# Score products of 28 and of 30 rows: one row count for all of them

## The chip, the cores and the metric

The kernel runs on one core of a Trainium2 chip. The metric is device time in microseconds (us). TensorE (PE in the profile) multiplies; it loads one operand as weights (PEld) and streams the other. VectorE (DVE), ScalarE (ACT) and GpSimd (POOL) do the elementwise work, and SyncE (SP) issues nearly all DMAs.

## The reference

Two attentions over the same x (2048 positions, 448 columns, 16 heads of 28), mixed by a gate. One looks at 8 positions at distance 2; the other, where nearly all of the time goes, is a full softmax attention:

```python
def _B_ref(x, wqkv, wo):
    qkv = (x @ wqkv).reshape(B, S, 3, H, Dh).transpose(2, 0, 3, 1, 4)
    q, k, v = qkv[0], qkv[1], qkv[2]
    scores = jnp.einsum("bhqd,bhkd->bhqk", q, k) * (Dh ** -0.5)
    p = _softmax(scores, axis=-1)
    o = jnp.einsum("bhqk,bhkd->bhqd", p, v)
    return o.transpose(0, 2, 1, 3).reshape(B, S, D) @ wo

g = _sigmoid((x * gate_w).sum(-1, keepdims=True))
return g * _A_ref(x, A_wqkv, A_wo) + (1 - g) * _B_ref(x, B_wqkv, B_wo)
```

`_A_ref` is the local attention. Everything is float32.

## The kernel before

[...]

**Three stages.** First x is multiplied with the weights (`project`, `project_halves`): the first ten tiles with all 128 rows of the array (line 320), the rest with two halves of 64 rows at a time (line 325). The high and low parts of queries and keys go to DRAM (`qk_hi`, `qk_lo`). The main stage, from about 248 us to 820 us, is the full attention with the local one beside it, and the last multiplies with `wo` (`op_tile`).

**Units, heads and strips.** A unit `u` is four heads (group `g`) by 512 queries, 16 units in all; a unit has 16 steps, one for each 128 keys, so 256 steps `st`. The four heads of a group lie in four strips of 32 partitions, head `h` in rows 32h to 32h + 27. Rows 28 and 29 of a strip are used in one kind of product: the keys' high tiles `KH` are filled with 1.0 (`init_kh`) before keys are loaded, and the queries' high tile `QH` gets two rows there (`load_nm`), the high and low part of the negative maximum of each query. So a high product of 30 rows yields scores with the maximum subtracted. The low tiles `QL` and `KL` have nothing in rows 28 and 29, and their products take 28 rows. `QH` and `QL` are made for each unit in a pool of two rotating buffers (`load_part`, called by `load_q` 4 steps before the unit, which then also loads the maxima's rows). There are three `KH` and two `KL` tiles, which are loaded again as groups come and go (`load_k`).

**Maxima's products.** The maxima are found beforehand from high by high products alone (`s1_mm`, line 149): those beside the projections take two strips at once (64 rows, the strip that is not wanted holding zeros in `QP`), those beside the main stage 28 rows. VectorE reduces each bank to its maximum (`s1_max`, line 155).

**A step.** `scores` writes products in a fixed order. A letter names the bank, a digit the term (0: `KH` by `QH`, 1: `KH` by `QL`, 2: `KL` by `QH`; `s0` to `s2` are the maxima's products):

```python
WITH = "10 20 s0 11 21 30 00 12 22 31 01 s1 s2 32 02".split()
```

Two ScalarE exponentials (line 1047) take two banks each. The three pairs of banks rotate: the pair that holds `s1` and `s2` in one step takes the products `30` and `00` in the next. Once no maxima are left, `ALONE` is the order, with the 12 products of the scores. After the products of a step, `do_av` (line 1008) multiplies the exponentials of the step before with the values, in 32 columns of the array for each head.

**The other engines.** Lists with costs and due steps spread the local attention's operations on GpSimd and VectorE over the steps; the same holds for the maxima's small steps (`max_parts`, `max_turn`, `max_store`). At the start, GpSimd sets constants and two `KH` tiles, VectorE clears three small tiles, and TensorE multiplies zeros (`warm`, line 220) until the first x and weights are there. `main_tiles`, called in the first step of the main stage, makes `KH2` and `KL1` in memory that the projections used.

Of the kernel before, what the change touches and what calls it, by code (L numbers as in the profile page):

```python
# [8 lines left out]
F32 = mybir.dt.float32  # L9
F32R = mybir.dt.float32r  # L10
# [5 lines left out]
S, D, H, DH = 2048, 448, 16, 28  # L16
NB, NJ, NG = 4, 16, 4
W, DIL = 8, 2
HALO = (W - 1) * DIL
SCALE = DH ** -0.5  # L20
NU = NG * NB
NMX = 192
# [3 lines left out]
def gated_mix_kernel(ctx: ExitStack, tc: tile.TileContext, xT, xn, gw, wA, wB, woAB, out):  # L26
    nc = tc.nc
# [3 lines left out]
    qk_hi = dram.tile([2 * D, S], F32R, name="qk_hi")  # L31
    qk_lo = dram.tile([2 * D, S], F32R, name="qk_lo")
# [11 lines left out]
    cp = ctx.enter_context(tc.tile_pool(name="cp", bufs=1))  # L44
    sp = ctx.enter_context(tc.tile_pool(name="sp", bufs=2))
# [27 lines left out]
    KL = [cp.tile([128, S], F32R, name="KL0")]  # L73
    MX = cp.tile([128, NMX], F32, name="MX")

    QP = [[cp.tile([128, 512], F32R, name=f"QP{i}{k}") for k in range(2)] for i in range(2)]

    def init_kh(t):
        nc.gpsimd.memset(t.bitcast(F32), 1.0)

    def pair(name):
        return pp.tile([128, 2, 512], F32, tag="P", name=name)

    half = {}
# [10 lines left out]
    def dma_r(dst, src):  # L99
        nc.sync.dma_start(dst.bitcast(F32), src.bitcast(F32))  # L100
# [4 lines left out]
            r = D + 112 * g + DH * h  # L105
            dma_r(t[32 * h:32 * h + DH, c], src[r:r + DH, c])

    def load_part(u, name, src):
        g, b = divmod(u, NB)
        t = sp.tile([128, 512], F32R, name=name)  # L110
        for h in range(4):
            r = 112 * g + DH * h
            dma_r(t[32 * h:32 * h + DH, :], src[r:r + DH, 512 * b:512 * b + 512])
        return t

    Qs = {}

    def load_q(u, low=True):
        Qs[u] = load_part(u, "QH", qk_hi), load_part(u, "QL", qk_lo)
        if low:  # L120
            load_nm(u)

    def load_nm(u):
        for i in range(2):
            dma_r(Qs[u][0][DH + i::32, :], nm[u][16 * i:16 * i + 16, :].rearrange("(h q) c -> h (q c)", h=4))
# [8 lines left out]
    def load_qhi(u):  # L134
        g, b = divmod(u, NB)
        qhis[u] = QP[u % 2]
        for h in range(4):
            r = 112 * g + DH * h
            dma_r(qhis[u][h % 2][32 * h:32 * h + DH, :], qk_hi[r:r + DH, 512 * b:512 * b + 512])

    def s1_mm(n, bank, half=False):
        u, i = divmod(n, 64)
        qs, kc, h = i // 16, i // 4 % 4, i % 4
        if u == 0:
            qs, kc = i // 8 % 4, 2 * (i // 32) + i // 4 % 2
        if i == 0 and u + 1 < NU:
            load_qhi(u + 1)
        r = slice(64 * (h // 2), 64 * (h // 2) + 64) if half else slice(32 * h, 32 * h + DH)
        nc.tensor.matmul(bank, qhis[u][h % 2][r, 128 * qs:128 * qs + 128],  # L149
                         KH[u // NB % 3][r, 512 * kc:512 * kc + 512], start=True, stop=True)  # L150

# [56 lines left out]

    for t in KH:
        init_kh(t)  # L210
    t0 = pair("t0")[:, 0, :]
    nc.vector.memset(t0, 0.0)
    nc.vector.memset(zt, 0.0)
    nc.vector.memset(omt, 0.0)

    zero = nc.const_aps.tensor(0.0, [128, 512], F32).bitcast(F32R)

# [8 lines left out]
    if True:  # L226
# [210 lines left out]
        nc.scalar.activation(zt, zt, AF.Exp)  # L437
        for t in QP[0]:
            nc.scalar.activation(t, t0, AF.Copy)
        r, t = xst[:, 0, 0:3, :], xst[:, 0, 3, :]  # L440
# [45 lines left out]
        for n, t in enumerate(tiles[:-1]):  # L486
# [4 lines left out]
            for w in splits:  # L491
                i, k = (n - splits[w][0]) * splits[w][1], splits[w][1]
# [19 lines left out]
            if n == 4:  # L512
                for t in QP[1]:
                    nc.scalar.activation(t, t0, AF.Copy)
# [20 lines left out]
            if parts and parts[0][0] <= n:  # L535
                _, u, t = parts.pop(0)
                max_store(u, max_turn(t))
            if finished and n < len(tiles) - 3:
                u = finished.pop(0)
# [10 lines left out]
            if n == 70:  # L550
                r = sp.tile([128, 32], F32, name="omr")
# [57 lines left out]
    def main_tiles():  # L609
        nonlocal mp, pm, maskt, actx, a1, a2, a3  # L610
        hctx.close()
        mp = ctx.enter_context(tc.tile_pool(name="mp", bufs=1))

        KH.append(mp.tile([128, S], F32R, name="KH2"))
        KL.append(mp.tile([128, S], F32R, name="KL1"))
        init_kh(KH[2])
        pm = ctx.enter_context(tc.tile_pool(name="pm", bufs=8))

        maskt = mp.tile([128, W, NJ, 2], F32, name="maskt")
        nc.gpsimd.memset(maskt, 0.0)  # L620
        for st, g, t, src in ((12, 2, KH[2], qk_hi), (30, 1, KL[1], qk_lo), (72, 2, KL[0], qk_lo),
                              (100, 3, KH[0], qk_hi), (136, 3, KL[1], qk_lo)):
            at("end", st, lambda g=g, t=t, src=src: load_k(g, t, src))
        for w in range(1, W):
            nc.gpsimd.memset(maskt[0:1, w, 0:DIL * w, :], -1e9 / SCALE)

        actx = ExitStack()
        a1 = actx.enter_context(tc.tile_pool(name="a1", bufs=1))
        a2 = actx.enter_context(tc.tile_pool(name="a2", bufs=2))
        a3 = actx.enter_context(tc.tile_pool(name="a3", bufs=5))  # L630
        for nme in ("k", "v"):
            for i in range(2):
                t = a1.tile([128, HALO + NJ, 56], F32, name=f"{nme}t{i}")
                kvt[nme, i] = t
# [4 lines left out]
    def a_load(c, nme):  # L639
# [3 lines left out]
        else:  # L643
            t = kvt[nme, c % 2]
            i = 1 if nme == "k" else 2
            nc.sync.dma_start(t[:, 0:HALO, :], a_prev[i][c, :, NJ - HALO:NJ, :])
            nc.sync.dma_start(t[:, HALO:, :], a_own[i][c])

    def a_score(c, w):
        if w == 0:  # L650
            Lt[c] = a2.tile([128, W, NJ, 2], F32, name="L", bufs=3)
        p = a3.tile([128, NJ, 56], F32, tag="prod", name="prod")
        nc.gpsimd.tensor_tensor(out=p, in0=qt[c], in1=kvt["k", c % 2][:, HALO - DIL * w:HALO - DIL * w + NJ, :],  # L653
                                op=ALU.mult)
# [10 lines left out]
    def a_softmax(c, i):  # L665
# [12 lines left out]
        elif i == 4:  # L678
            nc.scalar.activation(L, L, AF.Exp, scale=SCALE)  # L679
        elif i in (5, 6):  # L680
# [17 lines left out]
    def a_av(c, w, part):  # L698
# [3 lines left out]
        if part == 0:  # L702
# [3 lines left out]
            else:  # L706
# [3 lines left out]
                out=dst.rearrange("p j (h d) -> p j h d", d=DH),  # L710
                in0=kvt["v", c % 2][:, HALO - DIL * w:HALO - DIL * w + NJ, :].rearrange("p j (h d) -> p j h d", d=DH),
                in1=Lt[c][:, w, :, :, None].to_broadcast([128, NJ, 2, DH]), op=ALU.mult)
# [111 lines left out]
    def split_wo(k):  # L824
        if not wo:
            spare = [t[:, D * i:D * i + D] for t in (KH[1], KH[2], KL[0]) for i in range(4)] + [t[:, :D] for t in QP[0]]
            wo.extend((spare[:7], spare[7:]))
# [138 lines left out]
    for u in range(NU - 1):  # L966
        f = NJ * (u + 1)
        h = (16, 18)
# [50 lines left out]
    def scores(u, kt, cur):  # L1019
        g = u // NB  # L1020
        n = s1c[0]
        k = min(3, s1e - n)
        qh, ql = Qs[u]
        ks = slice(128 * kt, 128 * kt + 128)
        one, mine, other = ring
        ring[:] = (one, other, mine) if k else (other, one, mine)
        bank = {"1": one[:, 0, :], "2": one[:, 1, :], "3": mine[:, 0, :], "0": mine[:, 1, :],
                "s0": T1, "s1": other[:, 0, :], "s2": other[:, 1, :]}
        for tok in WITH if k else ALONE:
            if tok[0] == "s":  # L1030
                i = int(tok[1])
                if i < k:
                    s1_mm(n + i, bank[tok])
                if i == 0:
                    s1_max(n, 1, T1)
                elif i == 2 and k > 1:
                    s1_max(n + 1, k - 1, other[:, 0:k - 1, :])
                continue
            a, t = tok[0], int(tok[1])
            h = (int(a) + n) % 4  # L1040
            r = slice(32 * h, 32 * h + (DH + 2 if t == 0 else DH))
            nc.tensor.matmul(bank[a], (KH[g % 3], KH[g % 3], KL[g % 2])[t][r, ks], (qh, ql, qh)[t][r, :], start=(t == 0), stop=(t == 2))  # L1042
            if t == 2 and a in "20":
                if len(exps) < 5:
                    probs.append(pair("P"))
                p = probs[len(exps) % 5]
                e = nc.scalar.activation(p, one if a == "2" else mine, AF.Exp, scale=SCALE).ins  # L1047
                for o in exps[-5:-4]:
                    tc.declare_no_dep(e, o, query=mybir.DependencyQuery.ANY_SYNC,
                                      reason="PE has read what it wrote, and this one waits for PE")  # L1050
                for o in maxs[-4:]:
                    tc.declare_no_dep(e, o, reason="PE waited for it and the exponential waits for PE")
                exps.append(e)
                cur[(h + 3) % 4], cur[h] = p[:, 0, :], p[:, 1, :]
                yield len(cur)

    for u in range(NU):
        g, b = divmod(u, NB)
        for kt in range(NJ):
# [23 lines left out]
            if finished:  # L1083
                v = finished.pop(0)
                t = counted(lambda: max_parts(v, (lambda f: at("end", st + 1, f)) if v < NU - 1 else None))
# [25 lines left out]
    u = NU - 1  # L1111
# [30 lines left out]
```

## Time and profile before

| | |
|---|---|
| median of 3 runs | 896.43 us (896.38 to 896.9) |
| the profiled execution | 896.69 us, span of its records 894.9 us |
| TensorE busy | 890.2 us (99%) |
| VectorE, ScalarE, GpSimd busy | 740.5, 642.4, 638.7 us |
| exponentials (line 1047) | 512, 1023 ns each |
| maxima (line 155) | 470, 954 ns on average |
| weighted sums (line 1008) | 2048 records, 605 ns on average |

The span runs from the first record of the program to the last one; the execution's time has 1.8 us more around it. Matmuls are pipelined, and a record's duration holds its flight through the array and, for the first of a burst, its wait for weights: so durations add up to more than the time that passes, and the distance of two starts says more than a duration. A line of a timeline gives start and duration in us, engine, line, operation, the tiles written and read, shapes and a count; a group's line ends in busy us, mean ns, and idle time before it with what ended it.

### The profile page before, as it was taken

How to read it: one execution, taken by the hardware profiler on the slowest of the kernel's cores; microseconds unless marked ns; L12 is line 12 of the kernel's file. 1: busy time of each engine (PE TensorE's matmuls, PEld its weight loads, DVE VectorE, ACT ScalarE, POOL GpSimd, SP SyncE). 2: the span in 40 equal slices, each digit the busy share in tenths (PEclk: the TensorE clock that was granted, in tenths of full speed). 3: DMA queues.
4: the chain of work that ended last, by engine and by line, in shares of the span. 5: the costliest groups of instructions: out<-in, count | busy, mean ns of one | idle time of the engine just before them, and what ended most of it. 6: DMA issues, size and time to landing. Idle time of an engine off the chain costs nothing.

```text
span 894.9 us, 20516 instructions
## 1 busy us (share of the span) xinstructions
PE 890.2 (99%) x8312; PEld 533.4 (60%) x8312; DVE 740.5 (83%) x962; ACT 642.4 (72%) x766; POOL 638.7 (71%) x505
## 2 busy tenths in 40 slices
PE   9999999999999999999999999999999999999998
PEld 7889999999954444444444444444444444434997
DVE  6688999999979999999999999999999999832220
ACT  7456434343378898898988989989888898897220
POOL 1499846464459789998999989999999799701000
PEclk9999999999999999999999999999999999999999
DMA  8886403454372241225225222533121322437781
GB/s 267 277 267 186 151 12 84 135 142 121 103 248 66 89 139 46 67 61 156 71 56 143 86 62 86 128 96 98 45 64 32 89 43 49 104 78 214 192 265 52
DMA packets 114038, 104.51 MB, mean 117 GB/s; under 512 B 75240, under 2 KB 82280, under 8 KB 113160
## 3 DMA queue, kind: packets, MB, share of 16 engines
q1 hardware_dynamic: 113512, 102.42, 40.7%
q8 instruction: 65, 1.06, 0.5%
q10 hardware_dynamic: 432, 0.79, 0.3%
q14 instruction: 29, 0.24, 0.1%
HBM read 62.20 MB, written 40.96 MB: 115 GB/s over the span
## 4 chain that ended last, share of the span: by engine, by line
PE 99%; ACT 0%; issue 0%; ACTq 0%
PE T L1042 31%; PE av L1008 28%; PE r L325 15%; PE r L320 8%; PE T L886 8%; PE r L149 4%; PE T L149 4%; PE r L220 0%; PE av L472 0%; ACT P L1047 0%; ACT res L895 0%; ACT onhi L943 0%; ACT L L679 0%; ACTq L943 0%
## 5 line engine op out<-in xcount | busy, mean ns | idle before, releaser
L1047 ACT ACTIVATE P<-T 128x1024 f32<-128x1024 f32 x512 | 496.8, 1023 | 59.6 <-PE T L1042 57.9
L155 DVE TENSOR_REDUCE MX<-T 128x1 f32<-128x512 f32 x470 | 442.5, 954 | 31.7 <-PE T L149 13.7
L1008 PE MATMUL av<-P,V 128*32 128x512 f32 x2048 | 272.7, 605 | 0.0
L1042 PEld LDWEIGHTS T<-QH,KH 30*128 30x128 f32 x1024 | 92.2, 181 | 229.1 <-ACT P L1047 196.5
L149 PE MATMUL T<-KH,QP 28*128 28x512 f32 x704 | 220.3, 456 | 0.1
L1042 PE MATMUL T<-QH,KH 30*128 30x512 f32 x1024 | 211.7, 489 | 0.2 <-ACT P L1047 0.2
L171 DVE TENSOR_REDUCE MX<-r 128x2 f32<-128x1024 f32 x160 | 192.9, 1221 | 20.1 <-PE r L149 16.3
L1042 PE MATMUL T<-QH,KL 28*128 28x512 f32 x1024 | 185.7, 393 | 0.0
L1042 PE MATMUL T<-QL,KH 28*128 28x512 f32 x1024 | 184.3, 392 | 0.0
L653 POOL TENSOR_TENSOR prod<-qt,kt 128x896 f32<-128x896 f32 x64 | 135.4, 2116 | 6.4 <-DMA kt<-a_scr 6.4
L397 ACT ACTIVATE raw<-r 128x896 f32<-128x896 f32 (+1 forms) x62 | 57.1, 921 | 94.5 <-PE r L325 91.9
L149 PE MATMUL r<-KH,QP 64*128 64x512 f32 x320 | 114.5, 391 | 0.0
L714 POOL TENSOR_TENSOR oat<-oat,prod 128x896 f32<-128x896 f32 x48 | 101.2, 2109 | 2.0
L149 PEld LDWEIGHTS T<-KH,QP 28*128 28x128 f32 x704 | 86.1, 181 | 26.7 <-ACT P L1047 17.7
L325 PE MATMUL r<-wh,xh 64*128 64x448 f32 (+1 forms) x504 | 99.6, 363 | 0.0
L709 POOL TENSOR_TENSOR prod<-vt,L 128x896 f32<-128x896 f32 x56 | 95.3, 1702 | 0.3
L398 POOL TENSOR_TENSOR ast<-raw 128x448 f32<-128x448 f32 x47 | 54.3, 1154 | 56.4 <-ACT raw L397 43.9
L1042 PEld LDWEIGHTS T<-QL,KH 28*128 28x128 f32 x1024 | 94.3, 185 | 0.0
L1042 PEld LDWEIGHTS T<-QH,KL 28*128 28x128 f32 x1024 | 93.3, 183 | 0.2
L1008 PEld LDWEIGHTS av<-P,V 128*32 128x32 f32 x2048 | 40.3, 107 | 77.9 <-issue 65.4
L325 PE MATMUL r<-wl,xh 64*128 64x448 f32 (+1 forms) x441 | 79.0, 365 | 0.0
L325 PEld LDWEIGHTS r<-wh,xh 64*128 64x128 f32 x504 | 77.9, 185 | 0.1
(122 smaller groups left out, 1138.8 us busy)
## 6 DMA issues: line engine op xcount, KB each, us to landing
a_scr<-ast SPq DMA_DIRECT2D x24, 448.0 KB
qk_hi<-qkh SPq DMA_DIRECT2D x24, 256.0 KB
qk_lo<-qkh SPq DMA_DIRECT2D x24, 256.0 KB
rbc<-rs SPq DMA_DIRECT2D x64, 64.0 KB
QP<-qk_hi SPq DMA_DIRECT2D x64, 56.0 KB
KL<-qk_lo SPq DMA_DIRECT2D x16, 224.0 KB
QH<-qk_hi SPq DMA_DIRECT2D x64, 56.0 KB
QL<-qk_lo SPq DMA_DIRECT2D x64, 56.0 KB
```

Of the source, the lines that this page charges most:

```text
L149: nc.tensor.matmul(bank, qhis[u][h % 2][r, 128 * qs:128 * qs + 128], KH[u // NB % 3][r, 512 * kc:512 * kc + 512], start=True, stop=True)
L155: i = nc.vector.tensor_reduce(MX[:, n % NMX:n % NMX + k], bank, axis=X, op=ALU.max)
L171: nc.vector.tensor_reduce(m, PM[k], axis=X, op=ALU.max)
L320: nc.tensor.matmul(bank, ws[c][rows, k, t[4]:t[4] + 128], x, start=first, stop=last)
L325: nc.tensor.matmul(bank[:, 0:cols], x, ws[c][rows, k, 0:cols], start=first, stop=last)
L653: nc.gpsimd.tensor_tensor(out=p, in0=qt[c], in1=kvt["k", c % 2][:, HALO - DIL * w:HALO - DIL * w + NJ, :], op=ALU.mult)
L709: nc.gpsimd.tensor_tensor(out=dst.rearrange("p j (h d) -> p j h d", d=DH), in0=kvt["v", c % 2][:, HALO - DIL * w:HALO - DIL * w + NJ, :].r ...
L714: nc.gpsimd.tensor_tensor(out=ows[c % 2][:, :, 0:56] if w == W - 1 else oat[c], in0=oat[c], in1=oat[c, w], op=ALU.add)
L886: writes(bank, nc.tensor.matmul(bank[:, :D], src, wo[c][k], start=(first and k == ks[0] and i == 0), stop=(last and k == ks[-1] and i == 2)))
L1008: nc.tensor.matmul(av[32 * h:32 * h + 32, :], V[:, kt, 4 * g + h, :], tiles_[h], start=(kt == 0), stop=(kt == NJ - 1), skip_group_check=True)
L1042: nc.tensor.matmul(bank[a], (KH[g % 3], KH[g % 3], KL[g % 2])[t][r, ks], (qh, ql, qh)[t][r, :], start=(t == 0), stop=(t == 2))
L1047: e = nc.scalar.activation(p, one if a == "2" else mine, AF.Exp, scale=SCALE).ins
```

## The change

All products of the scores and of the maxima's 28-row form take 30 rows (`ROWS = DH + 2`). For that, rows 28 and 29 of the low tiles are made zero: `KL` by a memset of the whole tile on GpSimd, and `QL`, which becomes two fixed tiles used in turn, by a memset each on VectorE. Loads write rows 0 to 27 of a strip as before, so the zeros stay. The values do not change: in the low products one factor of the two added rows is zero, and in the maxima's products `QP` is zero there.

```diff
+ROWS = DH + 2
...
+    QL = [cp.tile([128, 512], F32R, name=f"QL{i}") for i in range(2)]
     QP = [[cp.tile([128, 512], F32R, name=f"QP{i}{k}") for k in range(2)] for i in range(2)]
...
+    def init_kl(t):
+        nc.gpsimd.memset(t.bitcast(F32), 0.0)
...
-    def load_part(u, name, src):
+    def load_part(u, t, src):
         g, b = divmod(u, NB)
-        t = sp.tile([128, 512], F32R, name=name)
...
-        Qs[u] = load_part(u, "QH", qk_hi), load_part(u, "QL", qk_lo)
+        Qs[u] = load_part(u, sp.tile([128, 512], F32R, name="QH"), qk_hi), load_part(u, QL[u % 2], qk_lo)
...
-        r = slice(64 * (h // 2), 64 * (h // 2) + 64) if half else slice(32 * h, 32 * h + DH)
+        r = slice(64 * (h // 2), 64 * (h // 2) + 64) if half else slice(32 * h, 32 * h + ROWS)
...
     for t in KH:
         init_kh(t)
+    init_kl(KL[0])
     t0 = pair("t0")[:, 0, :]
     nc.vector.memset(t0, 0.0)
     nc.vector.memset(zt, 0.0)
     nc.vector.memset(omt, 0.0)
+    for t in QL:
+        nc.vector.memset(t.bitcast(F32), 0.0)
...
         init_kh(KH[2])
+        init_kl(KL[1])
...
-            r = slice(32 * h, 32 * h + (DH + 2 if t == 0 else DH))
+            r = slice(32 * h, 32 * h + ROWS)
```

## The prediction

> **What bounds the kernel now.** I began with the page's busy times and its chain, which name the engine, then went to the windows, which say what the long stage is short of, and then to single steps in the timeline.
>
> ```profile
> PE 890.2 (99%) x8312; PEld 533.4 (60%) x8312; DVE 740.5 (83%) x962; ACT 642.4 (72%) x766; POOL 638.7 (71%) x505
> PE 99%; ACT 0%; issue 0%; ACTq 0%
> 275.00:770.00 495.00, 494.81 (x5060) 206.40 (x5060) 468.28 (x668) 441.45 (x496) 459.29 (x322) 1.00 0.31 81
> ```
>
> The first two lines say TensorE, and read alone they promise that anything that shortens a product shortens the kernel. The third line (columns: window, its length, busy PE, PEld, DVE, ACT, POOL, granted clock, DMA share, GB/s) warns against that: in the 495 us in which queries meet keys, VectorE is busy for 468.28 us, 94.6%. A busy PE record holds waiting too, so I looked at one step of that stage, in the order in which its products start.
>
> ```profile
> 503.93 1.22 DVE L155 TENSOR_REDUCE MX<-T 128x2 f32<-128x1024 f32 x1 [0.16 <-PE T L1042]
> 504.82 0.50 PE L1042 MATMUL T<-QH,KH 30*128 30x512 f32 x2
> 504.83 0.49 PE L149 MATMUL T<-KH,QP 28*128 28x512 f32 x1
> 505.16 0.40 PE L1042 MATMUL T<-QL,KH 28*128 28x512 f32 x2
> 505.20 0.50 PE L1042 MATMUL T<-QH,KH 30*128 30x512 f32 x2
> 505.38 0.41 PE L1042 MATMUL T<-QH,KL 28*128 28x512 f32 x2
> 505.55 0.40 PE L1042 MATMUL T<-QL,KH 28*128 28x512 f32 x2
> 505.62 0.40 PE L149 MATMUL T<-KH,QP 28*128 28x512 f32 x2
> 505.79 0.39 PE L1042 MATMUL T<-QH,KL 28*128 28x512 f32 x2
> 506.10 1.07 PE L1008 MATMUL av<-P,V 128*32 128x512 f32 x8
> 507.10 0.50 PE L1042 MATMUL T<-QH,KH 30*128 30x512 f32 x2
> ```
>
> The step lasts 507.10 - 504.82 = 2.28 us. Four heads lie in four strips of 32 rows, and each strip is a chain of its own: strips of the first two heads start at 504.82, 505.16, 505.38 and 505.62; the other two start their first high product only at 505.20. That product writes the pair of banks in which the step before left two products for the maxima, and the maximum over that pair ends at 503.93 + 1.22 = 505.15: TensorE waits for VectorE there, and the last products (505.79) hang on that start. A step without that wait looks like this:
>
> ```profile
> 516.16 0.50 PE L1042 MATMUL T<-QH,KH 30*128 30x512 f32 x2
> 516.38 0.49 PE L1042 MATMUL T<-QH,KH 30*128 30x512 f32 x1
> 516.49 0.40 PE L1042 MATMUL T<-QL,KH 28*128 28x512 f32 x2
> 516.50 0.40 PE L1042 MATMUL T<-QH,KH 30*128 30x512 f32 x1
> 518.28 0.50 PE L1042 MATMUL T<-QH,KH 30*128 30x512 f32 x2
> ```
>
> It takes 518.28 - 516.16 = 2.12 us. So the stage is set by two engines that take turns: TensorE's chain of products in the short steps, VectorE's maxima in the long ones.
>
> **The change part by part: the rows of the products.** These are the groups that change, and one that shows what 128 rows cost.
>
> ```profile
> L149 PE MATMUL T<-KH,QP 28*128 28x512 f32 x704 | 220.3, 456 | 0.1
> L1042 PE MATMUL T<-QH,KH 30*128 30x512 f32 x1024 | 211.7, 489 | 0.2 <-ACT P L1047 0.2
> L1042 PE MATMUL T<-QH,KL 28*128 28x512 f32 x1024 | 185.7, 393 | 0.0
> L1042 PE MATMUL T<-QL,KH 28*128 28x512 f32 x1024 | 184.3, 392 | 0.0
> 20.52 0.85 PE L320 MATMUL r<-xl,wh 128*128 128x512 f32 x3
> 21.21 1.09 PE L320 MATMUL r<-xh,wh 128*128 128x512 f32 x4
> ```
>
> 1024 + 1024 + 704 = 2752 products go from 28 to 30 rows; their columns (128 loaded, 512 streamed), banks, order and number stay. The means look as if 30 rows cost 489 ns against 392, but that is the place in the step and not the rows: the 28-row product at 504.83 stands in the same first place and took 0.49 us, too. The price of a row is read from starts in one strip. From 28 to 28 rows it is 505.38 - 505.16 = 0.22 us; 128 rows on the whole array take (21.21 - 20.52) / 3 = 0.23 us. Between 28 and 128 rows there are 100 rows and 0.01 us, so two rows more are worth under 1 ns a product, and even if all of it lay on the path, four in a row on each of 256 steps, it would be under 1 us. From below: could equal row counts save something? At 504.82 and 504.83 a 28-row product starts 0.01 us behind two 30-row ones, and at 516.49 and 516.50 a 30-row one starts 0.01 us behind two 28-row ones, so passing from one count to the other does not stop the queue. I take 0 for this part.
>
> One pair of starts does not fit at first sight: 505.16 - 504.82 = 0.34 us, 0.11 to 0.12 more than between later products, and it is the place where 30 rows are followed by 28. The loads explain it:
>
> ```profile
> L1042 PEld LDWEIGHTS T<-QH,KH 30*128 30x128 f32 x1024 | 92.2, 181 | 229.1 <-ACT P L1047 196.5
> L1008 PEld LDWEIGHTS av<-P,V 128*32 128x32 f32 x2048 | 40.3, 107 | 77.9 <-issue 65.4
> ```
>
> 128 columns take 181 ns and 32 take 107, so a column costs 74 / 96 = 0.77 ns and 128 columns cost 99 ns; a step's first product waits for its own load, since the weighted sums held the array before it, and a later one's load runs under the product ahead. 0.34 - 0.10 = 0.24 us is then the usual distance. [...]
>
> **The new tiles and memsets.** The low queries move from two rotating buffers to two fixed ones that alternate by unit, which is the same reuse distance: the DMAs that fill them still come a unit after the last reader, and their count and sizes stay. What is new is four memsets: two of 128x512 on VectorE and one of 128x2048 on GpSimd at the start, and one of 128x2048 on GpSimd when the main stage's tiles are made.
>
> ```profile
> 0.77 4.37 PE L220 MATMUL r<-const-float32-0.0 128*128 128x512 f32 x10 [0.77 <-PEq L1134]
> 0.91 0.48 DVE L212 MEMSET t<- 128x512 f32 x1 [0.91 <-PEq L1134]
> 1.25 3.54 POOL L83 MEMSET KH<- 128x2048 f32 x2
> 4.64 0.43 DVE L443 CAST xh<-V 128x512 fp32r<-128x512 f32 x1 [3.18 <-DMA V<-in_xT]
> 5.22 0.71 PE L320 MATMUL r<-xh,wh 128*128 128x512 f32 x2
> 252.50 1.81 POOL L83 MEMSET KH<- 128x2048 f32 x1 [1.86 <-PE av L472]
> 259.25 0.20 DVE L201 STREAM_TRANSPOSE nms<-nmt 128x32 f32<-128x32 f32 x1
> 261.60 2.13 POOL L653 TENSOR_TENSOR prod<-qt,kt 128x896 f32<-128x896 f32 x1 [6.44 <-DMA kt<-a_scr]
> ```
>
> VectorE's two cost 2 x 0.48 = 0.96 us and lie in the 3.18 us in which it waits for the first x: 0. The one in the main stage costs 1.8 us of GpSimd, in front of a gap of 6.44 us before its first product; the only other work it pushes back is a small subtraction that the transpose at 259.25 needs, and 252.50 + 2 x 1.81 = 256.1 leaves 3 us: 0. Without that cover it would be 1.8 us. The one at the start would run from 1.25 + 3.54 = 4.79 to 6.56 us, with GpSimd idle after it, but just when VectorE rounds the first x (4.64), on which the first real product (5.22) hangs. Its price has two ends. The low end is 0: the cast at 4.64 already ran beside a memset for its first 0.15 us, and took 0.43 us. The high end comes from casts late in the kernel:
>
> ```profile
> 783.15 1.29 POOL L947 TENSOR_TENSOR onlo<-on,onhi 128x512 fp32r<-128x512 f32 x1 [2.49 <-DVE KH L830]
> 783.29 1.40 DVE L829 CAST KH<-wor 128x448 fp32r<-128x448 f32 x1
> 809.76 0.43 DVE L862 CAST oahi<-oar 128x512 fp32r<-128x512 f32 x1 [7.40 <-DMA oar<-oa_scr]
> ```
>
> A cast of 448 columns took 1.40 us and ended at 784.69, 0.25 us after the GpSimd operation at 784.44, while one of 512 columns beside an idle GpSimd took 0.43. So a cast can be held until GpSimd is through; held by the new memset it would end at 6.56 + 0.25 = 6.81 instead of 5.07, 1.74 us late. I take 0, because the nearest row is the cast at 4.64, which met a memset and is no longer than the free one at 809.76, and keep 1.74 for the range.
>
> **Waits.** The low products now read rows that a memset wrote beside rows that a DMA wrote.
>
> ```profile
> L1042 PEldq EVENT_SEMAPHORE  x32: 51/51/51, 246.1 to 788.5; - x32
> ```
>
> For 3072 products this line has 32 separate wait instructions, although the 1024 high ones have several writers already. If each unit's four low-query and four low-key products got one more, it would be 16 x 8 x 51 ns = 6.5 us in the queue; I take 0, since the memsets lie long before any reader and the queue runs ahead of the array.
>
> **The sum.** Rows 0, fixed tiles 0, memsets 0 (up to 1.74), waits 0 (up to 6.5): the profiled execution would stay at 896.69 us (its span of 894.9 and 1.8 around it). It lies 0.26 us above the median of 896.43, so I forecast 896.5 us, with a range of its own from 895.5 to 898.2.
>
> **The rivals.** *Faster: the 0.11 us in front of the second product is the change of rows and not the load.* Equal rows would then take 0.11 us out of each of 256 steps, 28 us; but the long steps wait for VectorE, and in 495 us VectorE leaves only 26.7. In the third of the steps that are short it would be 256 / 3 x 0.11 = 9.4 us, 887 us; with VectorE taking back two thirds of that, 893.5. For it speaks the place of the 0.11 us, against it the load's slope and the starts 0.01 us apart.
>
> *Slower: GpSimd's memset holds the first cast.* It costs the 1.74 us, which is 898.2, and it opens a hole of as much between TensorE's zero products (which end at 5.14) and its first real ones. Those zero products went at 4.37 / 10 = 0.44 us each, the later ones at 0.23, so TensorE had sped up by then. If the hole takes that back for as long as the zero products needed, 4.37 / 0.44 = 10 products lose 0.2 us each: 2 us more, 900.2. It decides where the memset, and not the cast, goes first at 4.79 us. [...] Slower in another way: the waits in the queue, 903.
>
> *It does not do what it says* has no opening: the row slices are written out, and the zero rows are added with them.
>
> **How the numbers follow.** About 0.2% (1.8 us) is what a measurement of this kernel can tell from no change. No change gets 0.63; faster gets 0.15, all by the first rival; slower 0.22: 0.14 for the held cast with the slower products, 0.08 for the waits. From 893.0 to 900.5 the range takes in the forecast, the faster rival where VectorE takes most of it back, and the held cast; it leaves out the 887 and the 903, at most 2 in 10.
>
> **What would show it.** Right: products of 30 rows alone, whose means stay at about 392 ns in later places and 490 in the first; a long step still at 2.28 us with the second pair of heads 0.05 us behind the maximum; the cast at 4.6 us still 0.43 us long. Wrong: a distance of 0.23 instead of 0.34 us between a strip's first two products; a first real product later than 6 us; more wait instructions on the scores' line; or a VectorE share of the 495 us that moves away from 94.6%.

## The result, and the profile after

The changed kernel takes 898.57 us (median of 14 runs, 895.9 to 898.85) against 896.61 us for the kernel before (14 runs, 896.29 to 897.3): a ratio of 1.0014, with a 95% interval from 1.0006 to 1.0022. The ratio is taken over all runs; the medians alone give 1.0022. It is inside the 0.2% that the prediction counts as no change, but its interval leaves out 1. The profiled execution took 898.6 us with a span of 896.8, 1.9 us longer than the one before. The runs lie in groups: three at 895.9 to 896.0, one at 897.24, ten at 898.49 to 898.85. The kernel before has one group.

The busy times and the chain of the changed kernel's page, beside those shown of before:

```profile
PE 889.9 (99%) x8312; PEld 533.7 (60%) x8312; DVE 742.2 (83%) x964; ACT 642.5 (72%) x766; POOL 642.4 (72%) x507
PE 98%; DMA 1%; ACT 1%; issue 0%; ACTq 0%
```

VectorE has two instructions more and GpSimd two, the memsets. In the chain there is 1% of DMA and 1% of ScalarE that was not there: something at a place where TensorE had no work. The start of the changed kernel's timeline shows it (`xh` and `wh` are the high parts, x and the weights rounded to fp32r, `xl` and `wl` the low parts, what is left of them; a product of the two is made as three, `xh` by `wh`, `xl` by `wh` and `xh` by `wl`):

```profile
0.77 3.94 PE L227 MATMUL r<-const-float32-0.0 128*128 128x512 f32 x10 [0.77 <-PEq L1142]
1.24 3.54 POOL L85 MEMSET KH<- 128x2048 f32 x2
1.52 1.02 DVE L221 MEMSET QL<- 128x512 f32 x2
4.73 1.80 POOL L88 MEMSET KL<- 128x2048 f32 x1
4.81 2.00 DVE L450 CAST xh<-V 128x512 fp32r<-128x512 f32 x1 [2.27 <-DMA V<-in_xT]
6.96 0.90 PE L327 MATMUL r<-xh,wh 128*128 128x512 f32 x2 [2.25 <-ACT wh L454]
8.61 1.05 PE L327 MATMUL r<-xh,wl 128*128 128x512 f32 x2
9.47 1.05 PE L327 MATMUL r<-xh,wh 128*128 128x512 f32 x2
10.97 0.63 PE L327 MATMUL r<-xh,wl 128*128 128x512 f32 x2
11.43 0.61 PE L327 MATMUL r<-xh,wh 128*128 128x512 f32 x2
```

The new memset on GpSimd runs to 6.53. VectorE's first cast, 0.43 us before, takes 2.00 us and ends 0.28 us behind it. The first real product starts at 6.96 instead of 5.22, 1.74 us late. Its line names a ScalarE operation as what ended the wait, but ScalarE's first cast of the weights (line 454) was done at 4.99 in this trace; what ended last is VectorE's cast, at 6.81. Then pairs of products start 9.47 - 8.61 = 0.86 us apart, and later 0.46. The windows name the reason; the ninth column is the granted clock:

```profile
4.60:6.90 2.30, 0.11 (x1) 0.00 (x0) 2.05 (x2) 1.33 (x4) 1.94 (x2) 1.00 1.04 347
7.30:10.70 3.40, 3.40 (x9) 2.48 (x8) 3.34 (x8) 2.87 (x7) 0.00 (x0) 0.50 0.74 202
10.70:12.00 1.30, 1.30 (x7) 1.05 (x6) 1.27 (x4) 0.14 (x1) 0.00 (x0) 1.00 1.04 362
11.50:13.00 1.50, 1.50 (x8) 1.25 (x7) 0.79 (x2) 0.00 (x0) 0.00 (x0) 1.00 0.98 336
```

TensorE was idle for 2.25 us, and soon after it had work again it ran at half its clock for some 3.4 us, from 7.3 to 10.7. The eleventh real product is 3.15 us late (10.97; before, it started at 7.82); 0.45 us of that is caught up by about 20 us (places where TensorE had waited before: the largest, at 13.66, 14.24 and 15.45 us, are distances of 0.34, 0.29 and, for a pair, 0.66 us, which in the changed kernel are 0.22, 0.24 and 0.46), and from there to 230 us each product is 2.7 us late. The last product of the kernel is only 1.9 us late. So 0.8 us came back, and it came back in the main stage, bit by bit. The row of the low-query products gives its length, from first to last start, in the kernel before and then in the changed one:

```profile
L1042 PE MATMUL T<-QL,KH x1024: 384/392/417, 248.8 to 819.8; 28*128 28x512 f32 x171
```

```profile
L1050 PE MATMUL T<-QL,KH x1024: 382/388/417, 251.5 to 821.7; 30*128 30x512 f32 x171
275.00:770.00 495.00, 494.76 (x5064) 206.35 (x5060) 468.71 (x668) 442.16 (x497) 459.46 (x322) 1.00 0.31 81
```

571.0 us became 570.2, and the median duration went from 392 to 388 ns. VectorE's share of the 495 us is still 94.7%. The sum of the profiled executions: +2.7 at the start, -0.8 in the main stage, +1.9.

### The profile page after: what moved, and what is told of

It is laid out like the page before. It is cut to its first block, busy times and chain, and to the rows that moved or that the text cites. A ratio compares the mean times of both kernels' runs of the same rounds, so it can differ in the third digit from the quotient of the medians.

```text
span 896.8 us, 20520 instructions
## 1 busy us (share of the span) xinstructions
PE 889.9 (99%) x8312; PEld 533.7 (60%) x8312; DVE 742.2 (83%) x964; ACT 642.5 (72%) x766; POOL 642.4 (72%) x507
## 4 chain that ended last, share of the span: by engine, by line
PE 98%; DMA 1%; ACT 1%; issue 0%; ACTq 0%
PE T L1050 31%; PE av L1016 28%; PE r L332 15%; PE r L327 8%; PE T L894 8%; PE T L153 4%; PE r L153 4%; DMA V<-in_xT 1%; PE av L479 0%; ACT P L1055 0%; ACT xh L453 0%; ACT res L903 0%; ACT onhi L951 0%; ACTq L253 0%; ACT wh L454 0%
## 5 line engine op out<-in xcount | busy, mean ns | idle before, releaser
L153 PE MATMUL T<-KH,QP 30*128 30x512 f32 x704 | 220.9, 458 | 0.1
L1050 PE MATMUL T<-QH,KL 30*128 30x512 f32 x1024 | 185.8, 394 | 0.0
L1050 PE MATMUL T<-QL,KH 30*128 30x512 f32 x1024 | 183.1, 388 | 0.0
L153 PEld LDWEIGHTS T<-KH,QP 30*128 30x128 f32 x704 | 86.0, 181 | 26.3 <-ACT P L1055 16.2
L1050 PEld LDWEIGHTS T<-QL,KH 30*128 30x128 f32 x1024 | 94.0, 184 | 0.0
L1050 PEld LDWEIGHTS T<-QH,KL 30*128 30x128 f32 x1024 | 92.9, 182 | 0.2
```

## The experiments

My theory: the start lost 2.7 us through one GpSimd memset, in two terms (the held cast and the slow clock behind the hole), and the row counts of the products gave 0.8 us back. The rivals: a late start is simply taken up in the main stage, and rows do nothing; or it is the clearing as such, on whatever engine, that costs.

**The memset on another engine.**

```diff
-    init_kl(KL[0])
-    for t in QL:
+    for t in (*QL, KL[0]):
         nc.vector.memset(t.bitcast(F32), 0.0)
```

> The changed kernel with one line moved: the first memset of the low keys' tile (128x2048) is issued on VectorE behind its other small memsets and no longer on GpSimd; all products keep 30 rows. Theory (start and rows): GpSimd's memset held VectorE's first cast and cost 2.7 us by the 31st us, and 30 rows give 0.8 us back in the main stage; so this kernel takes 2.7 us less than the changed one, about 895.9, 0.5 to 0.8 us below the kernel before, the first cast takes 0.43 us again and the first real product starts at about 5.2 us. Rival (recovery): rows do nothing, the main stage only takes up a late start; then it takes what the kernel before takes, about 896.5. Rival (work at the start): it is the amount of clearing that costs and not its engine; then it stays near 898.5.

Measured: 895.97 us (11 runs, 895.38 to 896.81), a ratio to before of 0.9992 (0.9983 to 1.0001). Its timeline and its row of low-query products:

```profile
4.60 0.47 DVE L449 CAST xh<-V 128x512 fp32r<-128x512 f32 x1
5.21 0.47 PE L326 MATMUL r<-xh,wh 128*128 128x512 f32 x1 [0.26 <-DVE xh L449]
L1049 PE MATMUL T<-QL,KH x1024: 382/389/413, 249.2 to 819.5; 30*128 30x512 f32 x171
```

The same bytes are cleared, the cast is free, TensorE starts at 5.21, and the main stage is still 570.3 us: there is no late start left to take up, and the gain stays. The time and the groups at 897.2 and 898.5 went with the engine of one instruction.

**The rows taken back,** with the memsets as changed:

```diff
-        ... else slice(32 * h, 32 * h + ROWS)
+        ... else slice(32 * h, 32 * h + DH)
-            r = slice(32 * h, 32 * h + ROWS)
+            r = slice(32 * h, 32 * h + (ROWS if t == 0 else DH))
```

> The changed kernel with its tiles and memsets as they are, but with 28 rows again in the low products and in the maxima's products. Start and rows: the start stays 2.7 us late and the gain of the main stage goes, so about 899.2, 0.6 to 0.8 above the changed kernel. Recovery: the main stage takes up the late start in the same way, so 898.5 as the changed kernel.

Measured: 897.89 us in the median, in three groups: 896.4 to 896.9 (3 runs), 897.8 to 897.9 (3), 899.3 to 900.4 (5). The median of each group lies 0.6 to 0.9 us above that of a group of the changed kernel; the medians don't compare, since the groups are mixed in other shares. The profiled execution fell in the lowest one, which shows a cast that gets in first:

```profile
4.61 0.46 DVE L450 CAST xh<-V 128x512 fp32r<-128x512 f32 x1 [2.06 <-DMA V<-in_xT]
4.73 2.08 POOL L88 MEMSET KL<- 128x2048 f32 x1
L1050 PE MATMUL T<-QL,KH x1024: 385/392/416, 248.8 to 819.7; 28*128 28x512 f32 x171
```

Here x landed 0.2 us earlier than in the changed kernel, the cast came while the memset before was running (until 4.79), and the new memset waited for the cast: it took 2.08 us instead of 1.80. The main stage is 570.9 us. The kernel with both edits:

> Both edits at once: the low keys' first memset on VectorE, and 28 rows in the low and the maxima's products. Only the fixed low tiles and the clearing are left of the change. Both theories say 896.5, as the kernel before. Beside the kernel that differs from it in the rows alone, start and rows says 0.6 to 0.8 us more here, recovery says the same time.

It took 896.48 us (896.2 to 897.03), 0.5 us more than the first one, with this row:

```profile
L1049 PE MATMUL T<-QL,KH x1024: 385/392/402, 248.7 to 819.7; 28*128 28x512 f32 x171
```

571.0 us. With a free start, rows alone are worth 0.5 us in the medians and 0.7 us in the main stage's records: both the recovery and the clearing as such are out. The rows of the low-query products agree: with 30 rows in the high and the low products (the changed kernel, this memset on VectorE, and further down `warm(19)`, 250.7 to 821.1, and rows of 30, 30, 28) the main stage takes 570.2 to 570.4 us, whether it begins at 248.9 or at 251.5, and in the four kernels with 30 and 28 rows 570.9 to 571.0.

**No hole for the clock.** `warm(10)` becomes `warm(19)`.

> The changed kernel with 19 in place of 10 products of zeros ahead of the first real one, so that TensorE has no hole from 4.7 to 7.0 us. The theory that the late start has two terms, the held cast (1.7 us) and products at half speed behind the hole (1.4 us), says that the second goes: the first real product still starts at about 7.0 us, the granted clock between 8.6 and 12 us is 1.0 instead of 0.69, and the time falls by 1.0 to 1.4 us to about 897.3. The rival (VectorE, itself late, sets the pace of the products there, whatever TensorE's speed) says 898.5.

Measured: 897.41 us (896.94 to 897.9), in one group. Its timeline and window:

```profile
4.79 2.03 DVE L450 CAST xh<-V 128x512 fp32r<-128x512 f32 x1 [2.25 <-DMA V<-in_xT]
7.82 0.62 PE L327 MATMUL r<-xh,wh 128*128 128x512 f32 x2
8.28 0.63 PE L327 MATMUL r<-xl,wh 128*128 128x512 f32 x2
8.60:12.00 3.40, 3.40 (x16) 2.74 (x15) 3.31 (x8) 2.15 (x6) 0.00 (x0) 1.00 0.89 282
```

The cast is held as before, the clock stays at 1.00, pairs are 0.46 us apart from the first on, and 1.2 us are gone. One thing was not as expected: the zero products went at half speed for longer (in the changed kernel they start 0.43 us apart up to 3.89 us and 0.22 from there on; here 0.43 up to 4.32 and 0.33 on average behind it) and the last of them started at 7.6, so the first real product started at 7.8 and not at 7.0. The slow products behind the hole are thus a term of their own, and VectorE, itself late, was not what paced them.

**Which rows?** All of the next four have the low keys' tile cleared on VectorE; the edits are those row slices again.

> The low keys' first memset on VectorE; the low products take 30 rows, the maxima's products beside the main stage 28. All three theories of the 0.6 to 0.7 us that the main stage became shorter: (count) each product of 30 rows is a little faster than one of 28, so three quarters of the gain come from the 2048 low ones and one quarter from the 704 maxima's; (equality) the gain needs that all rows are equal, so little of it is here; (low products) the whole gain is here. From the first to the last low-query product the main stage then takes 570.4 to 570.5 us by count, 571.0 by equality, 570.3 by low products (571.0 in the kernel before, 570.2 in the changed one). Time 896.0 to 896.5, by itself too close to tell.

> The low keys' first memset on VectorE; the maxima's products take 30 rows, the low products 28. From the first to the last low-query product: by count 570.8 us, by equality 571.0, by low products 571.0. Time about 896.3 to 896.5.

> The low keys' first memset on VectorE; all products of the scores and maxima take 28 rows, the high ones too, so the negative maxima are not added to the scores (this part is left out). Equality: as good as 30 rows for all, 570.3 us from the first to the last low-query product and a time of about 895.9. Count (30 rows are faster than 28 in themselves): 571.0 us or a little more, as 1024 more products have 28 rows, 571.2 and 896.6.

> The low keys' first memset on VectorE; all products of the scores and the maxima take 32 rows, the whole strip: the two more rows of the queries' tiles hold zeros (the high queries lie in two fixed tiles, too, cleared by two more ScalarE copies of 0.6 us in the first stage). Equality: the same as 30 rows for all, 570.3 us in the main stage and 895.9 plus up to 1.1 for the copies. A full strip is faster: by the slope from 28 to 30 rows another 0.6 us less, 569.6 us in the main stage and a time of 895.3 plus the copies' part.

The rows of the low-query products, in the same order:

```profile
L1049 PE MATMUL T<-QL,KH x1024: 382/389/422, 248.9 to 819.1; 30*128 30x512 f32 x171
```

```profile
L1049 PE MATMUL T<-QL,KH x1024: 384/392/417, 249.3 to 820.3; 28*128 28x512 f32 x171
```

```profile
L1049 PE MATMUL T<-QL,KH x1024: 382/388/421, 248.9 to 819.2; 28*128 28x512 f32 x171
```

```profile
L1050 PE MATMUL T<-QL,KH x1024: 382/390/414, 249.2 to 819.8; 32*128 32x512 f32 x171
```

| rows of high, low, maxima's products | main stage, us | median time, us (11 runs each) |
|---|---|---|
| 30, 30, 28 | 570.2 | 896.01 |
| 30, 28, 30 | 571.0 | 896.52 |
| 28, 28, 28 | 570.3 | 895.80 |
| 32, 32, 32 | 570.6 | 896.81 |

It is not the number of rows: 28 throughout is as good as 30 throughout. It is not the maxima's products either. Of the three theories, low products fits the first two kernels and equality the third; count fails at the third. What fits the first three is a narrower equality: the high and the low products of the scores must have the same rows, whatever the maxima's have. The gain is 0.7 to 0.8 us over 256 steps, 3 ns a step. Products that follow each other in a strip, or that add into the same bank, are candidates for where a change of rows costs something; which of the two it is was not tried. In the first kernel rows still change between a maxima's product and its neighbours in a strip, which write other banks, at no cost that can be seen; that speaks for the bank, but does not show it. With 32 rows throughout only half of the gain is there, which the narrower equality doesn't explain, and I have no reason for it; the time of that kernel also holds two ScalarE copies at the start, and its projections run 0.4 us late.

**How long is the cast held?** First, the memset on GpSimd in four pieces of 512 columns:

> The changed kernel with GpSimd's first memset of the low keys' tile cut into four of 512 columns, back to back. If the cast waits only for the GpSimd operation that is running when it comes, it is held at most 0.5 us (a quarter of 1.77 and 0.25 behind it), ends before 5.4 us, and the time is 896.0 to 896.5. If GpSimd keeps VectorE out as long as its next operation follows at once, the cast ends at 6.8 us as in the changed kernel and the time stays near 898.5.

The profiled execution took 896.11 us and reads as the first theory said, with the cast held for one piece:

```profile
4.68 0.87 DVE L451 CAST xh<-V 128x512 fp32r<-128x512 f32 x1 [2.13 <-DMA V<-in_xT]
4.74 2.21 POOL L88 MEMSET KL<- 128x512 f32 x4
```

But the median of 11 runs is 898.62 us (896.11 to 899.96), no better than with one piece. So two more: the memset twice, and in sixteen pieces.

> The changed kernel with the low keys' tile cleared twice on GpSimd, back to back, so that GpSimd writes until 8.3 us and not 6.5. If VectorE's cast gets in after the operation that was running when it came, the second one costs nothing and the time is that of the changed kernel, 898.5. If GpSimd can keep VectorE out over the border between two operations, the cast is held 1.77 us longer and the time is 900.3 or more.

> The changed kernel with the same memset on GpSimd in sixteen pieces of 128 columns, about 0.11 us each. Held by one piece alone, the cast is at most 0.15 us late and the time 896.0 to 896.3; held over the borders it ends near 6.8 us and the time is 898.5, as with the single memset and, in the median, with four pieces.

Twice: 898.56 us (895.79 to 899.87), as the changed kernel; profiled at 897.14 us:

```profile
0.77 4.60 PE L228 MATMUL r<-const-float32-0.0 128*128 128x512 f32 x10 [0.77 <-PEq L1143]
4.65 2.17 DVE L451 CAST xh<-V 128x512 fp32r<-128x512 f32 x1 [2.11 <-DMA V<-in_xT]
4.74 3.83 POOL L88 MEMSET KL<- 128x2048 f32 x2
6.97 0.70 PE L328 MATMUL r<-xh,wh 128*128 128x512 f32 x2 [1.59 <-ACT wh L455]
7.61 0.74 PE L328 MATMUL r<-xl,wh 128*128 128x512 f32 x2
8.18 0.62 PE L328 MATMUL r<-xh,wl 128*128 128x512 f32 x2
6.97:9.30 2.33, 2.33 (x9) 1.69 (x10) 2.33 (x5) 1.99 (x5) 1.60 (x1) 1.00 0.74 166
```

The cast ends at 6.82, behind the first memset, and the second one waits for it (the two take 3.83 us, those of the high keys' tiles before them 3.55). This trace also shows a held cast without the slow clock (granted clock 1.00 from 6.97 on, pairs 0.64 and 0.57 us apart as at the start of the kernel before), and it lies in the group at 897.2. But its hole is shorter, 1.59 us: the zero products, which start at 0.77 in both, end at 5.37 here and at 4.71 in the changed kernel; the last four of them, from 3.46 on, take 1.91 us here and 1.25 there. Sixteen pieces: 897.56 us, in two groups of five runs, 895.6 to 896.1 and 899.0 to 899.4; profiled in the upper one:

```profile
4.71 2.71 DVE L451 CAST xh<-V 128x512 fp32r<-128x512 f32 x1 [2.16 <-DMA V<-in_xT]
4.73 2.40 POOL L88 MEMSET KL<- 128x128 f32 x16
```

Here the cast was held over all sixteen. So it is one operation where they are 1.8 us long, one of four in one trace, and sixteen of sixteen in another: whether VectorE gets in at a border between two short GpSimd operations isn't settled by these runs. What is settled is that smaller pieces are no cure.

**No GpSimd work beside the first cast.** GpSimd clears only the first high keys' tile at the start, VectorE the second one, and the low keys' tile is cleared by GpSimd beside the projections.

> All products with 30 rows; at the start GpSimd clears only the first high keys' tile (done at 3.05 us), VectorE the second one in the time in which it waits for x, and the low keys' tile is cleared by GpSimd at the projections' tile 50. No GpSimd operation is left where the first cast runs. If the hold of 0.15 us that the cast has in the kernel before (until 4.79) matters, the first real product starts 0.1 to 0.2 us earlier and the time is about 895.8; if something else (the weights' cast at 4.99, the zero products until 5.1) comes last there, it is that of the kernel with the memset on VectorE, 895.97.

```profile
4.60 0.40 DVE L449 CAST xh<-V 128x512 fp32r<-128x512 f32 x1
5.21 0.72 PE L326 MATMUL r<-xh,wh 128*128 128x512 f32 x2
```

895.99 us (895.38 to 896.23), a ratio of 0.9990 to the kernel before (0.9981 to 0.9999). The cast ends at 5.00 instead of 5.07, the first product does not start earlier: 5.21 as before. The gain over the kernel before is under 0.2%, but its interval leaves out 1; that of the kernel with the memset on VectorE (895.97) just takes 1 in. Between these two there is nothing to choose.

## Why the prediction was right or wrong

**The time and the range.** 896.5 us was forecast, 898.57 came, inside the range of 893.0 to 900.5 and 0.4 us above the forecast's own range. That it still counts as no change is luck: two terms that the sum held at 0 came out at +2.7 and -0.8 us and partly cancel. What happened at the start is the rival *slower: GpSimd's memset holds the first cast*, with its place, its 1.74 us (measured: 1.74) and its slow products behind the hole, and one of the forecast's signs of being wrong came, a first real product later than 6 us (6.96). Its price of 898.2 to 900.2 holds the measured time, and the range had been drawn to take it in. The mistake is in its chance of 0.14.

**The step that failed** is the memsets' term, where I took 0 of 0 to 1.74 "because the nearest row is the cast at 4.64, which met a memset and is no longer than the free one". That row could not tell: the cast came 0.15 us before that memset ended, and a held cast ends about 0.28 us after, which makes 0.43 us, the time of a free one. The cast at 783.29, held for its whole wait and 0.25 us more, was the better row. It also mattered by how little the order is decided: in these traces the cast that came at 4.61 was not held by the new memset, those at 4.65 and 4.81 waited for all of it.

**The hole.** I gave the clock's fall to half speed 10 products at 0.2 us. It was 3.15 - 1.74 = 1.4 us at the eleventh product. The trace shows the fall to 0.50 behind 2.25 us without work, and a slow stretch of some 3.4 us. What decides whether it comes isn't settled: the clock fell behind the holes of 2.25 us (changed kernel) and 2.77 us (sixteen pieces, 0.66 from 8.6 to 12 us), and not behind those of 1.59 us (the memset twice) and 0.49 us (four pieces), both 1.00 there. That would fit a limit somewhere between 1.59 and 2.25 us, which is an estimate from these four traces and not shown by itself: the zero products also come to full speed at different times in different traces (0.22 us apart from 3.89 us on in the changed kernel, still 0.42, from 4.32 to 4.74, in the kernel before), and which of the two counts was not tried.

**Rows: 0 was forecast, -0.8 us came.** The bound from above was right, the one from below too coarse: starts read to 0.01 us cannot show 3 ns, and 256 steps make 0.8 us of them. The starts 0.01 us apart were also those of products in different strips (the first maxima's product takes the strip of head `n % 4`, banks 1 and 2 those of the next two heads), and so say nothing of a change of rows within one. The faster rival had the right thing, unequal rows, at 0.11 us a step, nearly forty times too much. The 0.34 us between a strip's first two products are still there with equal rows (507.16 and 507.50 in the changed kernel), so they are not the change of rows; that they are the load, as argued, fits but was not tested:

```profile
507.16 0.50 PE L1050 MATMUL T<-QH,KH 30*128 30x512 f32 x2
507.50 0.39 PE L1050 MATMUL T<-QL,KH 30*128 30x512 f32 x2
507.55 0.50 PE L1050 MATMUL T<-QH,KH 30*128 30x512 f32 x2
```

**Right:** VectorE's two memsets (1.02 us) lie in its wait for x. The main stage's memset is hidden: the gap before GpSimd's first product shrank from 6.44 to 3.94 us, and the transpose that needs the subtraction behind it came 2.3 us later than that. The queue has 32 wait instructions as before:

```profile
256.96 1.81 POOL L88 MEMSET KL<- 128x2048 f32 x1
259.43 0.21 POOL L196 TENSOR_TENSOR nmt<-nmv,nmt 128x16 fp32r<-128x16 f32 x1
261.95 0.20 DVE L205 STREAM_TRANSPOSE nms<-nmt 128x32 f32<-128x32 f32 x1
263.58 2.11 POOL L661 TENSOR_TENSOR prod<-qt,kt 128x896 f32<-128x896 f32 x1 [3.94 <-DMA kt<-a_scr]
L1050 PEldq EVENT_SEMAPHORE  x32: 51/51/51, 248.8 to 790.5; - x32
```

**Open:** why the changed kernel's runs fall into groups is shown by one trace for each group (its own at 898.6, those of the four pieces at 896.1 and of the memset twice at 897.1), but not run by run; three of the ten runs at 898.5 to 898.85 list a granted clock of 1.0, the other seven 0.997 or 0.998. A listed 1.0 does not rule out slow products at the start, though. In the kernel before, this window reads 1.00 while the ten zero products in it start 0.43 us apart, as slow as the pairs of 0.86 us:

```profile
0.70:5.00 4.30, 4.23 (x10) 3.19 (x10) 0.91 (x4) 2.84 (x5) 3.98 (x4) 1.00 0.67 181
```

So those three may be runs whose TensorE had not come to full speed before the hole; no trace shows one, so this stays open. Why 32 rows give half, and what in a change of rows costs 3 ns, is open too.

## What to carry to other kernels

An instruction on an idle engine isn't free when it can hold up the one that the critical engine waits for (here a GpSimd memset of 1.80 us, and a first product 1.74 us late): put such clearing on an engine that is waiting itself, or where nothing on the path runs (895.97 and 895.99 us here, against 898.57). In a start-up, price a delay twice: the wait (1.74 us here), and the clock that the hole behind it may cost (1.4 us here). Where an effect repeats hundreds of times, read its size from a stage's length (here 0.8 us over 256 steps) and not from one step.

## What the runs showed of the hardware that was not expected

A GpSimd memset of 1.80 us, which reads nothing, held a VectorE cast until 0.28 us behind its end (2.00 us instead of 0.43 in the changed kernel), while a VectorE memset (2 x 0.51 us at 1.52, beside GpSimd's memsets, and the same at 3.66 with GpSimd idle, in the kernel without GpSimd work beside the first cast) and a VectorE subtraction of two tiles (0.69 us from 5.10 on in the kernel with 28 rows, beside GpSimd's memset, and 0.69 us without it in the kernel before) ran at their usual speed. Rows of 30 in the high and 28 in the low products of the scores cost some 3 ns a step of 12 to 15 products, against 30 or 28 in both. And TensorE's clock halved for 3.4 us after a hole of 2.25 us. Over a span of 896.8 us that makes a mean of 0.998, so the listed clocks, 0.997 or 0.998 in seven of the changed kernel's 14 runs and 1.0 in the others, say that not every execution has this fall.
